# The column sums of WQ behind the first tile's query products, with a new order table

## Chip, cores and metric

The kernel runs on one core of a Trainium2 chip. The metric is the device time of one execution in microseconds (us); several runs are given by their median. The engines are TensorE (PE, with its weight loads PEld), VectorE (DVE), ScalarE (ACT), GpSimd (POOL) and SyncE (SP), which issues most DMAs.

## What is computed

The input x has 2048 rows of 512 columns and is normalised row by row first. Two branches work on the result xn, and the output is x + s * silu(B).

```python
xn = _layernorm(x)                       # no scale, no bias
# A: linear attention, 32 heads of 16
q, k, v = split(xn @ wqkv)               # wqkv: 512 x 1536
pq, pk = phi(q), phi(k)                  # phi(t) = (t + 1 if t > 0 else exp(t)) + 1e-6
s = (pq @ (pk^T v)) / (pq . sum(pk) + 1e-6) @ wo       # per head
# B: shift mixer and MLP
h = gelu(layernorm(xn) @ w1)             # its four column quarters shifted by +1, -1, +2, -2 rows
x1 = xn + shifted(h) @ w2
B = x1 + gelu(layernorm(x1) @ w3) @ w4   # w3: 512 x 1376
out = x + s * silu(B)
```

## The kernel before

**Tiles.** The rows are 16 tiles of 128, in four groups ("quarters") of four tiles; the 512 columns are four chunks of 128. Every fp32 product is made of three products of rounded parts: each operand is split into a rounded high half (`...h`, made on ACT by `rounded`, L522) and a low rest (`...l`, a subtraction on DVE), and `products` (L514) issues high x high, high x low and low x high. Products of one 128 x 128 block by 512 columns go into one PSUM bank. There are eight banks: four of tag `acc`, which the sums `G` (`g`) take, and four of tag `mm`, for everything else.

**Normalisation behind the product.** The first quarter's keys and queries are made from the raw x: `project` (L758) multiplies the transposed x by WK or WQ, 12 products for one tile (four chunks by three). The mean is taken off afterwards: (x - mean) W = xW - mean * (sum of W's rows). `sums` (L766) makes that sum: three additions of the four chunks on DVE (`wqt`), the rounding to `wqmh` on ACT and `wqml` on DVE, two products with a matrix of ones into a PSUM bank (`qsum`), and an ACT copy with sign changed (`qneg`). `query` (L867) then makes `qt` = mean * `qneg` + product on DVE, which is also what frees the tile's PSUM bank, and `feature_q` (L856) goes on with ACT and two DMAs. For the keys it is the same with `ksum`, `wneg` and `kt` (`feature_k`, L828).

**The written order around the change.** At the start come WK's loads, the loads of x, the key products of tiles 0 to 3 (banks k0 to k3), `sums(WK)` and the key features. Then WQ is loaded and split (L1542, L1543) and `sums(WQ, bank("qsum"), qneg)` stands at L1544. Then comes the list `ORD` (L1591): the loads of the second quarter's transposed x (`lu`), the query of tile 0 (`q 0`), `hal`, `x 1`, the query of tile 2 (`q 2`), W1's loads, the sums `g 0`, and so on to the stage `h`, the mixer's first product with W1.

**The emitted order** is made by a planner, `Plan` (L89). Every call of the helpers adds an operation with an estimate of its time; `deadlines` (L259) gives each product of PE a nominal time in written order and each other operation a due time, counted back from the products that need it. `nudged` (L253) then shifts single due times by a table: in `SOONER` (L1745) each pair is an operation's number and a count, and the operation is due by a quarter of a us times the count sooner. `emit` (L296) plays the program through and lets on each engine the operation go that can start first, and among such the one that is due first. PE may take products from up to 12 us ahead. So an operation's place in the queue of its engine follows from the written order, the estimates and the table together, and each engine then works its queue strictly in that order.

Of the kernel before, what the change touches and what calls it, by code (L numbers as in the profile page):

```python
# [430 lines left out]
def linear_attn_gated_by_mixer(  # L431
# [52 lines left out]
    def piece(name, dt=F32):  # L484
        return pl.new("p", name, dt, PIECE)[:, :512]

    def rounds(name):

        return piece(name + "h", F32R), piece(name + "l", F32R)
# [4 lines left out]
    def bank(name):  # L494
        return pl.new("mm", name, F32, 512)[:, :]
# [18 lines left out]
    def products(ps, terms, start=True, stop=True, more=False, behind=None):  # L514

        ms = []
        for sh, sl, mh, ml in terms:
            ms += [(sh, mh), (sh, ml), (sl, mh)]
        for n, (s, m) in enumerate(ms):
            pl.mm(ps, s, m, start and n == 0, stop and n == len(ms) - 1, more=more, behind=None if n else behind)  # L520

    def rounded(hi, lo, full, src=None):  # L522

        pl.act(hi, src or full, AF.Copy)
        split(lo, full, hi)
# [36 lines left out]
    def mean(mv, i):  # L562
        return mv[:, 2 * i:2 * i + 1]
# [191 lines left out]
    def ut(b, c, a, z):  # L755
        return tuple(t[:, a:z] for t in UT[b][c])

    def project(ps, i, ws, cs):  # L758
        b, j = divmod(i, QT)
        a = 2 + j * P  # L760
        products(ps, [ut(b, c, a, a + P) + ws.chunk(c) for c in cs], 0 in cs, NC - 1 in cs)
# [4 lines left out]
    def sums(w, ps, out):  # L766

        t, r = piece(f"{w.name}t"), w.raw
        pl.tt(t, r[0], r[1], ALU.add)
        pl.tt(t, t, r[2], ALU.add)  # L770
        pl.tt(t, t, r[3], ALU.add)
        ts = rounds(w.name + "m")
        rounded(*ts, t)
        for n, v in enumerate(ts):
            pl.mm(ps, onesr.all, v, n == 0, n == 1)
        pl.act(out, ps, AF.Copy, scale=-1.0)
# [79 lines left out]
    def feature_q(i, t):  # L856
        if i >= LATE:
            pl.soon(pl.store(pqd[i].all, t))
            return
        e, r = (piece(f"q{n}{i}") for n in "er")  # L860
        pl.act(by_block(e), by_chunk(t), AF.Relu, scale=col(ns1, i))
        pl.act(by_block(r), by_chunk(t), AF.Relu, scale=col(rs1, i))
        pl.act(e, e, AF.Exp, scale=-1.0)
        pl.soon(pl.store(pqd[i].all, r))
        pl.soon(pl.gather(pqd[i].all, e))

    def query(i):  # L867
        ps = bank(f"q{i}")
        project(ps, i, WQ, range(NC))
        t = piece(f"qt{i}")  # L870
        pl.stt(t, qneg, mean(mv1, i), ps, ALU.mult, ALU.add)
        feature_q(i, t)
# [628 lines left out]
    wneg, qneg = piece("wneg"), piece("qneg")  # L1501
# [39 lines left out]
        feature_k(i, ks[i])  # L1541
    WQ = Weights("wq", wqkv[0])  # L1542
    WQ.split()  # L1543
    sums(WQ, bank("qsum"), qneg)  # L1544
    def scaled(b):
        for j in range(QT):
            if b == 1:
                load_rows(b * QT + j)
            else:
                load_x(b * QT + j)  # L1550
        scale_x(b * QT, QT)
# [54 lines left out]
    def load_w1():  # L1606
        HELD.append(Weights("w1", w1))

    DO = {"wc": lambda: HELD[0].center(by_dma=True), "lu": lambda: load_u(1, 1), "hal": halos, "lw": load_w1, "x": scaled, "kq": keys_queries, "w1": w1_for, "st": stats_of, "g": gram, "mix": mixer, "w2": prepare_w2,
          "a": spread_a, "h": split_halo, "m2": mix2, "u": make_u, "k": key, "q": query, "T": forms_kq}  # L1610
    for what, *args in ORD:
        pl.early = SOON.get(what, 0.0)
# [52 lines left out]
    for b in range(NQ):  # L1665
# [77 lines left out]
                gate(b, QT - 1, r, a, TH, xr=xr[QT - 1], whole=a > 0)  # L1743

    SOONER = (  # L1745
# [18 lines left out]
    )  # L1764
    pl.emit(first=6.0, lead={"p": 14.0, "w": 14.0}, reserve={"p": 20, "w": 1}, window=12.0,
            ahead=6.0, table=SOONER)
# [37 lines left out]
```

## Time and profile before

| what | value |
|---|---|
| median of 3 runs | 503.85 us (503.77 to 504.27) |
| the profiled execution's own time | 503.29 us |
| its span in the profile | 501.5 us |
| granted PE clock, mean | 0.999 |
| PE, PEld busy | 494.1 us, 442.1 us |
| DVE, ACT, POOL busy | 443.4 us, 387.4 us, 82.7 us |
| DMA | 116.69 MB, mean 233 GB/s |

A row of a timeline gives the start in us from the span's start, the duration in us, engine, line, operation, what it writes and reads by the program's names (without buffer numbers), its shape, and in brackets how long the engine stood idle before it and what ended that. In PE's rows the durations overlap, as products are pipelined; the distance from one start to the next tells how fast they go. A row of the view of waits gives who waited for whom, the total in us, how many times, and the longest. Nearly every product is recorded at L151, DVE's additions and subtractions at L198, ACT's work at L173, since helpers issue them; the tile names tell them apart.

### The profile page before, as it was taken

How to read it: one execution, taken by the hardware profiler on the slowest of the kernel's cores; microseconds unless marked ns; L12 is line 12 of the kernel's file. 1: busy time of each engine (PE TensorE's matmuls, PEld its weight loads, DVE VectorE, ACT ScalarE, POOL GpSimd, SP SyncE). 2: the span in 40 equal slices, each digit the busy share in tenths (PEclk: the TensorE clock that was granted, in tenths of full speed). 3: DMA queues.
4: the chain of work that ended last, by engine and by line, in shares of the span. 5: the costliest groups of instructions: out<-in, count | busy, mean ns of one | idle time of the engine just before them, and what ended most of it. 6: DMA issues, size and time to landing. Idle time of an engine off the chain costs nothing.

```text
span 501.5 us, 9471 instructions
## 1 busy us (share of the span) xinstructions
PE 494.1 (99%) x3102; PEld 442.1 (88%) x3102; DVE 443.4 (88%) x944; ACT 387.4 (77%) x859; POOL 82.7 (16%) x97
## 2 busy tenths in 40 slices
PE   8999999999999999999999999999999999999996
PEld 6777887898888888899899999999899998999995
DVE  6899999999699896999999998998899979987364
ACT  6899799766888795977767688957799778977451
POOL 1267123131221022020100011200020200201101
PEclk9999999999999999999999999999999999999999
DMA  7959984479976799989776698988598886896805
GB/s 254 337 138 256 321 256 128 99 157 279 335 219 160 219 307 214 288 232 330 256 250 214 218 326 229 267 255 241 192 275 277 226 207 216 283 329 189 200 1 126
DMA packets 86989, 116.69 MB, mean 233 GB/s; under 512 B 8864, under 2 KB 41148, under 8 KB 86940
## 3 DMA queue, kind: packets, MB, share of 16 engines
q1 hardware_dynamic: 77004, 98.00, 60.2%
q0 software_dynamic: 9936, 18.09, 20.9%
q8 instruction: 24, 0.39, 0.3%
q14 instruction: 25, 0.20, 0.1%
HBM read 73.70 MB, written 32.91 MB: 213 GB/s over the span
## 4 chain that ended last, share of the span: by engine, by line
PE 90%; ACT 4%; DMA 3%; DVE 1%; SPq 0%; issue 0%; ACTq 0%
PE a L151 14%; PE pb L151 10%; PE h L151 9%; PE g L151 9%; PE pbk L151 7%; PE acc L151 6%; PE pe L151 5%; PE pbm L151 5%; PE pbs L151 5%; PE pek L151 3%; PE uc L151 3%; PE pa L151 2%; PE pes L151 2%; PE pem L151 2%; PE pak L151 2%; PE q L151 1%
## 5 line engine op out<-in xcount | busy, mean ns | idle before, releaser
L230 POOL DMA_DIRECT2D th<-in_x x14 | 12.3, 930 | 166.3 <-DMA w_t<-w4t 75.3
L230 POOL DMA_DIRECT2D o<-x x16 | 13.8, 866 | 63.9 <-DVE o L198 42.7
L178 ACT ACT_TABLE_LOAD x18 | 23.1, 1283 | 0.3
L230 POOL DMA_DIRECT2D zacc<-kr x16 | 16.9, 1058 | 35.6 <-DVE kr L208 16.8
L173 ACT ACTIVATE gf<-gf 128x256 f32<-128x256 f32 (+1 forms) x48 | 21.9, 468 | 0.3
L652 POOL TENSOR_TENSOR rs<-w,nhalf 128x4 f32<-128x4 f32 (+2 forms) x10 | 15.8, 1643 | 36.8 <-DVE w L203 36.8
L230 POOL DMA_DIRECT2D e<-x1d x12 | 10.6, 1083 | 63.3 <-DVE e L198 59.7
L173 ACT ACT_TABLE_LOAD x11 | 14.1, 1283 | 2.2 <-issue 1.0
L173 ACT ACTIVATE ht<-ht 128x512 f32<-128x512 f32 x16 | 9.8, 625 | 6.7 <-DVE ht L198 6.2
L208 DVE SCALAR_TENSOR_TENSOR kr<-kt,kr 128x512 f32<-128x512 f32 x16 | 10.9, 684 | 4.3 <-ACT kt L173 4.2
L198 DVE TENSOR_TENSOR th<-th,so 128x512 f32<-128x512 f32 (+1 forms) x17 | 11.0, 655 | 3.6 <-ACT th L173 3.6
L198 DVE TENSOR_TENSOR e<-a,e 128x512 f32<-128x512 f32 (+1 forms) x17 | 9.8, 588 | 4.8 <-PE a L151 4.8
L173 ACT ACTIVATE y<-o,nm,rs 128x512 f32<-128x512 f32 x16 | 11.8, 806 | 2.6 <-DVE nm L208 2.6
L646 DVE BATCH_NORM_STATS2 st<-o 128x6 f32<-128x512 f32 x16 | 10.8, 686 | 3.3 <-DMA o<-x 3.3
L173 ACT ACTIVATE p<-pe 128x256 f32<-128x256 f32 x20 | 7.6, 382 | 7.4 <-PE pe L151 7.4
L198 DVE TENSOR_TENSOR gf<-pa,p 128x256 f32<-128x256 f32 x20 | 8.4, 422 | 5.1 <-PE pa L151 4.5
L173 ACT ACTIVATE x<-x,nm,rs 128x512 f32<-128x512 f32 x16 | 12.9, 804 | 0.0
L173 ACT ACTIVATE th<-e 128x512 f32<-128x512 f32 (+1 forms) x12 | 7.1, 606 | 7.5 <-DVE e L198 7.4
L198 DVE TENSOR_TENSOR ht<-h,abc 128x512 f32<-128x512 f32 x16 | 10.9, 686 | 1.2 <-PE h L151 1.0
L173 ACT ACTIVATE p<-pb 128x256 f32<-128x256 f32 x20 | 7.5, 377 | 5.4 <-PE pb L151 5.3
L208 DVE SCALAR_TENSOR_TENSOR pq<-pq,rd 128x512 f32<-128x512 f32 x16 | 10.9, 678 | 0.1
L1413 DVE TENSOR_REDUCE den<-qz 128x32 f32<-128x512 f32 x16 | 10.8, 681 | 0.1
(1868 smaller groups left out, 2288.5 us busy)
## 6 DMA issues: line engine op xcount, KB each, us to landing
w_s<-in_w SPq DMA_DIRECT2D x34, 256.0 KB, 5.1
w_t<-w4t SPq DMA_DIRECT2D x26, 256.0 KB, 6.2
w_b<-w4d SPq DMA_DIRECT2D x24, 256.0 KB, 4.7
x<-in_x SPq DMA_DIRECT2D x16, 256.0 KB, 6.2
zacc<-kr POOLq DMA_DIRECT2D x16, 256.0 KB, 4.9
o<-x POOLq DMA_DIRECT2D x16, 256.0 KB, 4.7
x1d<-o SPq DMA_DIRECT2D x16, 256.0 KB, 3.2
xt<-in_xt SPq DMA_DIRECT2D x15, 256.0 KB, 6.3
```

The source lines that it names most:

```text
L151: lambda: nc.tensor.matmul(out.get(), lhs.get(), rhs.get(), start=start, stop=stop, skip_group_check=more))
L173: nc.scalar.activation(out.get(), src.get(), func, scale=get(scale), **kw)
L178: op.warm = lambda: nc.scalar.activation(self.scr[1].get(), self.scr[0].get(), func)
L198: self.vec(eng, out, [a, b], lambda: self.e(eng).tensor_tensor(out.get(), a.get(), b.get(), op=op), True)
L208: lambda: self.nc.vector.scalar_tensor_tensor(out.get(), a.get(), get(s), b.get(), op0=op0, op1=op1),
L230: lambda: self.nc.gpsimd.dma_start(out.get(), get(src), accum_op=ALU.add))
L646: pl.add("DVE", .62, .69, [xv], [st], lambda: nc.vector.bn_stats(st.get(), xv.get()))
L652: lambda: g.tensor_tensor(out.get(), src.get(), nh.get(), op=ALU.pow))
L1413: pl.add("DVE", .6, .68, [t], [den], lambda: nc.vector.tensor_reduce(den.get(), t.get().rearrange("p (h d) -> p h d", d=DH), axis=AX.X, op ...
```

## The change

The call of `sums` for WQ is taken out of the main line and put into `query`, for tile 0, between the tile's 12 products and the DVE operation that uses `qneg`. The operations of the loads `lu` and of the 12 products so get numbers lower by 8, those of the sum higher by 16; all others keep theirs. The table `SOONER` is replaced: 163 pairs for 181. 35 pairs are the same in both, 68 operations have another count, 78 are nudged only before and 60 only after. The first lines of both tables are shown.

```diff
     def query(i):
         ps = bank(f"q{i}")
         project(ps, i, WQ, range(NC))
+        if i == 0:
+            sums(WQ, bank("qsum"), qneg)
         t = piece(f"qt{i}")
         pl.stt(t, qneg, mean(mv1, i), ps, ALU.mult, ALU.add)
         feature_q(i, t)
...
     WQ = Weights("wq", wqkv[0])
     WQ.split()
-    sums(WQ, bank("qsum"), qneg)
     def scaled(b):
...
     SOONER = (
-        0, 16, 2, 377, 19, 8894, 26, 3270, 31, 261, 34, 64, 36, 38809, 42, 3243, 43, 155, 55, 33, 62, 32, 72, 16,
-        83, 16, 86, 58, 87, 64, 94, 64, 97, 64, 117, -64, 121, 9, 134, 13, 152, 16, 165, 8, 168, 35, 170, 568,
-        171, 512, 174, 31, 176, 16, 178, 32, 199, 32, 203, -32, 213, 31, 253, -16, 266, 70, 277, 3, 278, 57,
...
+        2, 309, 19, 38290, 23, 20, 24, 16, 26, 2469, 31, 130, 36, 38310, 42, 1201, 43, 154, 54, 5, 55, 36, 62, 32,
+        70, 16, 83, 15, 86, 58, 89, 8, 97, 130, 121, 18, 127, 114, 170, 248, 171, 515, 174, 62, 176, 19, 177, 64,
+        191, 32, 203, -71, 213, 10, 253, -83, 273, 61, 278, 28, 280, 33, 297, 16, 305, -32, 316, 457, 320, 83,
...
     )
```

28 rows, old and new, of the table SOONER are left out of this document.

## The prediction

> **What bounds the kernel now.** I read the page first, then the view of TensorE's waits, then the engines' timelines from 17 to 37 us, and last the busy time by stretches.
>
> ```profile
> span 501.5 us, 9471 instructions
> PE 494.1 (99%) x3102; PEld 442.1 (88%) x3102; DVE 443.4 (88%) x944; ACT 387.4 (77%) x859; POOL 82.7 (16%) x97
> PE 90%; ACT 4%; DMA 3%; DVE 1%; SPq 0%; issue 0%; ACTq 0%
> ```
> TensorE (PE) is busy for 99% of the span and makes 90% of the chain that ended last. Time can come only from places where PE stands still. The view of PE's waits has two rows:
>
> ```profile
> PE warm L151 <- POOL ones L548: 1.7, 1, 1.7
> PE qsum L151 <- ACT wqmh L173: 0.8, 1, 0.8
> ```
> The first is the start. The second is the sum that the change moves: the first `qsum` product waits for `wqmh`, the rounded sum of WQ's rows. PE's timeline there:
>
> ```profile
> 20.64 0.39 PE L151 MATMUL q<-wq_3h,u_3l 128*128 128x512 f32 x1
> 20.87 0.40 PE L151 MATMUL q<-wq_0h,u_0h 128*128 128x512 f32 x1
> ...
> 21.58 0.39 PE L151 MATMUL q<-wq_1h,u_1h 128*128 128x512 f32 x1
> 22.79 0.50 PE L151 MATMUL qsum<-wqmh,onesr 128*128 128x512 f32 x1 [0.82 <-ACT wqmh L173]
> 23.13 0.40 PE L151 MATMUL q<-wq_1l,u_1h 128*128 128x512 f32 x1
> 23.36 0.40 PE L151 MATMUL q<-wq_1h,u_1l 128*128 128x512 f32 x1
> ...
> 24.75 0.40 PE L151 MATMUL q<-wq_3h,u_3l 128*128 128x512 f32 x1
> 24.98 0.39 PE L151 MATMUL qsum<-wqml,onesr 128*128 128x512 f32 x1
> ```
> Products of 512 columns start 0.23 us apart (20.64, 20.87). After 21.58 the next would start at 21.81; it starts at 22.79, **0.98 us late**, and the one behind it follows after 0.34 instead of 0.23, 0.11 more. So the stall costs 0.98 + 0.11 = 1.09 us. Two things in these rows matter for the change. The `qsum` product already stands behind all twelve products of the first query tile (the last of them at 20.64) and four of the next: the emitting order is not the written one. And eight products that had long been ready stood behind it (23.13 to 24.75). What made it late:
>
> ```profile
> 19.05 0.74 DVE L208 SCALAR_TENSOR_TENSOR kt<-wneg,mv,k 128x512 f32<-128x512 f32 x1
> ...
> 20.59 0.69 DVE L198 TENSOR_TENSOR wqt<-wqt,wq_s 128x512 f32<-128x512 f32 x1
> 21.19 0.15 DVE L203 TENSOR_SCALAR mv<-sx 128x1 f32<-128x1 f32 x1
> 21.25 0.68 DVE L198 TENSOR_TENSOR x0l<-x,x0h 128x512 fp32r<-128x512 f32 x1
> 21.85 0.74 DVE L208 SCALAR_TENSOR_TENSOR kt<-wneg,mv,k 128x512 f32<-128x512 f32 x1
> ...
> 23.83 0.69 DVE L198 TENSOR_TENSOR wqml<-wqt,wqmh 128x512 fp32r<-128x512 f32 x1
> ```
>
> ```profile
> 21.50 0.62 ACT L173 ACTIVATE sq<-x 128x512 f32<-128x512 f32 x1
> ...
> 22.12 0.62 ACT L173 ACTIVATE wqmh<-wqt 128x512 fp32r<-128x512 f32 x1
> ...
> 25.42 0.60 ACT L173 ACTIVATE qneg<-qsum 128x512 f32<-128x512 f32 x1 [0.56 <-PE qsum L151]
> ```
> `wqmh` ends at 22.12 + 0.62 = 22.74. There is a second condition that the waits view does not name. PSUM has four `mm` banks; k0 to k3 hold them all, q0 and q2 take the first two that VectorE (DVE) frees with a `kt` (q2, at 20.87, behind the `kt` of 19.05), and the sum takes the next: the `kt` at 21.85 ends at 22.59. An earlier `wqmh` alone would have won 22.74 - 22.59 = 0.15 us.
>
> **The change part by part.**
>
> The eight operations of the sum stay: three additions and `wqml` on DVE (0.69 us each), `wqmh` and `qneg` on ScalarE (ACT, 0.62 and 0.60), two products (0.23). No DMA, table load or tile is added. Busy time: 0.
>
> The move itself. In the written order the sum goes behind 12 products, so its due times fall by 12 x 0.23 = 2.8 us, as do those of the additions that feed it. PE's emission already had it later than that, so the move says only that the additions may go later. Best case: both `qsum` products come behind the eight ready products of the second tile, which without the stall end their starts at 24.75 - 1.09 = 23.66. Then `wqmh` (22.74) and the bank (22.59) are long there: gain 1.09 us. Worst case: the product is again emitted the moment the planner thinks it ready, and the stall stays: 0. These are the two ends for this edit.
>
> What is late next. A PE that is 1.09 us earlier at 25 us runs into operands that do not come earlier with it, since they come from ACT and DVE:
>
> ```profile
> 24.00:34.00 10.00, 10.00 (x45) 7.92 (x45) 9.47 (x26) 9.25 (x21) 6.11 (x6) 1.00 0.67 163
> 34.00:44.00 10.00, 10.00 (x45) 7.81 (x43) 9.78 (x21) 9.55 (x27) 8.64 (x7) 1.00 0.84 175
> 44.00:54.00 10.00, 10.00 (x45) 8.12 (x45) 9.96 (x19) 10.00 (x26) 3.47 (x4) 1.00 1.09 287
> ```
> The columns behind the stretch are its sum, PE, PEld, DVE, ACT and POOL. DVE is busy 9.47, 9.78 and 9.96 of 10 us and ACT 9.25, 9.55 and 10.00: no room to be earlier, only to be ordered otherwise. The next operands that are just in time:
>
> ```profile
> 29.25 0.61 ACT L173 ACTIVATE k2h<-kr 128x512 fp32r<-128x512 f32 x1
> ...
> 32.08 0.61 ACT L173 ACTIVATE w1mh<-w1t 128x512 fp32r<-128x512 f32 x1
> ...
> 34.97 0.61 ACT L173 ACTIVATE k1h<-kr 128x512 fp32r<-128x512 f32 x1
> ```
>
> ```profile
> 30.44 0.85 PE L151 MATMUL g<-k2h,x2h 128*128 128x512 f32 x3
> 31.12 0.40 PE L151 MATMUL g<-k2l,x2h 128*128 128x512 f32 x1
> ...
> 33.10 0.40 PE L151 MATMUL w1m<-w1mh,onesr 128*128 128x512 f32 x1
> ...
> 35.99 0.87 PE L151 MATMUL g<-k1h,x1h 128*128 128x512 f32 x3
> ```
> `k2h` ends at 29.86 and its first product starts at 30.44, 0.58 later; `w1mh` 32.69 and 33.10: 0.41; `k1h` 35.58 and 35.99: 0.41. From `wqmh`'s end to its product passed 22.79 - 22.74 = 0.05, so a product can follow its operand by that. The lead that survives all three is 0.41 - 0.05 = 0.36 us. Of 1.09 us won at 22 us, 0.73 would be lost again by 36 us.
>
> One place of the Trainium skill speaks on whether a stall of PE lasts at all: "TensorE: Matmul & The Clock Gate", section "Back-to-back issue gap", gives a sustained 131 ns per 512-column product in a real kernel against about 216 for a single one. By that PE would make up 1.09 us in about 11 products, and removing the stall would bring nothing: 503.85. The rows above disagree: behind the stall the products start 0.23 us apart as before it (23.13, 23.36), so nothing is made up.
>
> The new table. It has 163 pairs in place of 181; 35 are as before, the others nudge due times by new amounts, all over the program. It issues nothing new, but it may exchange neighbours on every queue, SP's first loads included (entries 19 to 43), and it was drawn up for another order. The trace of before cannot show what it does. Bounds from the nearest rows: a gain is limited by PE's other halts, of which these are the largest:
>
> ```profile
> 242.27 0.40 PE L151 MATMUL acc<-w_0h,f_0l 128*128 128x512 f32 x1
> 242.66 0.39 PE L151 MATMUL pb<-yt40h,w_b 128*128 128x256 f32 x1
> 242.88 0.28 PE L151 MATMUL pb<-yt40l,w_b 128*128 128x256 f32 x1
> ```
>
> ```profile
> 379.57 0.28 PE L151 MATMUL a<-w_t,f_1a 128*128 128x256 f32 x1
> 379.95 0.39 PE L151 MATMUL pe<-yb222h,w_s1h 128*128 128x256 f32 x1
> 380.17 0.28 PE L151 MATMUL pe<-yb222l,w_s1h 128*128 128x256 f32 x1
> ```
> At 242.27 a 512-column product is followed after 0.39 and the next 256-column one after 0.22 instead of 0.23 and 0.12: 0.26 us. At 379.57 it is 0.38 and 0.22 instead of 0.12 twice: 0.36 us. Together 0.62. A loss is bounded by the price of one misplaced product, the 1.09 us of `qsum`; two new ones of its kind make 2.2. I take 0, the middle of -0.6 and +2.2 being no better founded: before shows one such wait in 500 us, so the nearest row for a finished order is few waits.
>
> Sum: 503.85 - 0.36 + 0 = **503.5 us**. The profiled execution took 503.29 us, 501.5 of it span; by the same sum it would take 502.9. The median of the three runs, 503.85, stands 0.56 above it, and the forecast is set against the median.
>
> **The rivals.**
>
> *Little is won (forecast).* The stall goes or shrinks, the lead is lost at the next just-in-time operands, 503.5. Or the change does not do what it says: as PE's queue had the sum behind the first tile already, the stall stays, 503.85. Both are within 0.2% (1.0 us), which is about what a measurement of this kernel can tell from no change. For it: the surviving 0.36 and the full DVE and ACT. Against: a new order can break up exactly those three places. Chance 0.40, of which 0.02 for PE making up a stall (503.85).
>
> *The lead is kept: faster.* The table puts `k2h`, `w1mh` and `k1h` early enough by letting DVE's additions of `wqt` go later, and the halts at 242 and 380 go too: 503.85 - 1.09 - 0.62 = 502.1; the lead alone is 502.8. For it: the additions are what stood ahead of the others on DVE at 20.59. Against: 1.0 us needs nearly all of the 1.09, through a stretch where DVE and ACT are full for 30 us. Chance 0.28.
>
> *The moved additions make key products late: slower.* Place: DVE's queue from 23.8 to 31 us. There stand `wqml` and what `k2l` needs, and PE's product on `k2l` follows at 31.12. Its row:
>
> ```profile
> 29.90 0.69 DVE L208 SCALAR_TENSOR_TENSOR k2l<-kr,k2h 128x512 fp32r<-128x512 f32 x1 [0.39 <-ACT k2h L173]
> ```
> `k2l` ends at 30.59, 0.53 ahead of its product. Starts of DVE instructions of this kind are 0.60 apart (20.59 to 21.19). If all of the three additions and `wqml` slide by their 2.8 us into this stretch, `k2l` comes 4 x 0.60 = 2.4 us later, less the slack of 0.53 - 0.05: +1.9, 505.8; with three of them +1.3, 505.2. It decides from two additions on (1.2 us against a slack of 0.48). Against it: what leaves DVE's queue at 18 to 21 us makes room there for others, so the total does not grow. With a like misplacement elsewhere in the run, by the price of two waits, 506.0. Chance 0.32.
>
> **How the numbers follow.** Within 0.2%: 0.40; faster: 0.28; slower: 0.32. Signs both ways hold most of the chance; the forecast's own range is 502.9 to 504.3 (its two ends with 0.5 of spread between runs: 503.77 to 504.27). The whole range leaves out a tenth on each side: from 502.1, the fast rival's price, to 506.0, the slow one's.
>
> **What would show it.**
>
> ```profile
> 42.74 0.40 PE L151 MATMUL h<-u_0h,w_0h 128*128 128x512 f32 x1
> ```
> This is the first product of `h`, the next stage. The move right: no wait of PE on `wqmh`, and eight products of the second query tile without a hole. The term 0.36 right: new short waits of PE at `k2h`, `k2l`, `w1mh` or `k1h` between 28 and 37 us, and the first product of `h` earlier than 42.74 by 0.2 to 0.5 us. Wrong to the fast side: that product earlier by 0.9 or more and no later wait. Wrong to the slow side: rows of PE waiting of 0.5 us and more on DVE or a DMA, anywhere. The table's 0 is wrong if the time from the first `h` product to the end differs from now by more than 0.6.

## Result and profile after

In six runs of each kernel, the changed kernel took **502.07 us** (501.63 to 502.89), the one before 504.06 (503.77 to 504.44). The ratio is **0.9963, 95% interval 0.9953 to 0.9973**: faster by 0.37%, 1.9 us. That is not the forecast case (within 0.2%); it is the size of the fast rival (502.1). The experiments show that its mechanism was another. Three of all executions below took 812 to 984 us, whatever the kernel, and stand in no ratio.

The device time is longer than the span of the instructions in the profile, and no view shows what lies between the two. In before this part is 1.96 to 1.98 us (medians of its executions beside three groups of runs), in after 1.72 and 1.71. So some 0.25 of the 1.9 us lies where no row below can show it.

The page of the changed kernel follows; its profiled execution took 502.89 us, the slowest of the six.

```profile
span 501.2 us, 9464 instructions
PE 494.3 (99%) x3102; PEld 442.2 (88%) x3102; DVE 440.9 (88%) x944; ACT 388.9 (78%) x859; POOL 84.9 (17%) x97
PE 88%; DMA 8%; SPq 1%; ACT 1%; issue 0%; DVE 0%; POOL 0%; DVEq 0%
PE a L151 15%; PE pb L151 11%; PE h L151 9%; PE pbk L151 7%; PE g L151 7%; PE acc L151 6%; PE pe L151 6%; DMA w1t<-in_w 5%; PE pbm L151 5%; PE pbs L151 4%; PE uc L151 3%; PE pek L151 3%; PE pa L151 3%; PE pem L151 2%; PE pes L151 2%; PE pak L151 2%
```

Busy times are as before. New is the chain that ended last: DMA has 8% of it instead of 3%, and 5% are the gathers of W1 (`w1t<-in_w`). The view of PE's waits (total, times, longest in us) says the same:

```profile
PE w1m L151 <- ACT w1mh L173: 0.6, 1, 0.6
PE h L151 <- ACT w_1h L173: 0.2, 1, 0.2
```

The wait of `qsum` on `wqmh` is gone, and two new ones stand at W1. PE's timeline at the sum (start, duration):

```profile
23.56 0.40 PE L151 MATMUL q<-wq_3l,u_3h 128*128 128x512 f32 x1
23.81 0.51 PE L151 MATMUL qsum<-wqmh,onesr 128*128 128x512 f32 x1
24.15 0.40 PE L151 MATMUL q<-wq_3h,u_3l 128*128 128x512 f32 x1
```

```profile
23.14 0.62 ACT L173 ACTIVATE wqmh<-wqt 128x512 fp32r<-128x512 f32 x1
```

Seven of the eight ready products now stand ahead of the sum. `wqmh` has slid too, from 22.74 to 23.76 at its end, so the product still only just finds it: 23.81 is 0.02 behind the usual distance and the next 0.11 more. In this execution the stall of 1.09 us shrank to 0.13. But the stall differs from execution to execution with the same queues, counted as the prediction did (hole and 0.11 behind it): in the seven executions that have before's queues up to 60 us (before, before_again, before_tail, before_to60, before_60_349, before_mid, before_late) it was 1.09, 0.45, 0.69, 1.16, 1.10, 0.35 and 0 us (median 0.69), in the four with after's (after, after_again, after_to60, after_tail) 0.13, 0.44, 0.38 and 0. It depends on when PE comes to the product, and so on its earlier halts: in before PE is ready for the product at 21.81 and waits until 22.79, in before_late it comes to it only at 24.17, when `wqmh` has been ready since 23.90, and doesn't wait. The 1.09 us of the prediction stand near the top of this range.

Then the stage `h`:

```profile
43.02 0.40 PE L151 MATMUL h<-u_0h,w_0h 128*128 128x512 f32 x1
...
43.95 0.63 PE L151 MATMUL h<-u_0h,w_0l 128*128 128x512 f32 x2
44.80 0.49 PE L151 MATMUL h<-u_1h,w_1h 128*128 128x512 f32 x1 [0.22 <-ACT w_1h L173]
```

Here the first `h` product is not earlier than 42.74 but 0.28 later, and the one on `w_1h` stands 0.38 late behind two products (0.85 instead of 0.47). Yet the kernel is faster.

**One measure for all runs.** For every execution the table gives PE's *standing time*: the start of a product less the usual distances of all products ahead of it (0.232 us for 512 columns, 0.118 for 256, 0.112 and 0.027 for the two small kinds). Two places are met with the same work done in all kernels: the first `h` product (167 products, 36.25 us of work) and the 271st product (60.18). The third place is at 481 us of work. "End" is from PE's last product's end to DVE's last. The letters tell whose queues (before's, after's) run up to 60 us, up to 490 us, and to the end.

| run | queues | at first `h` | at 60 of work | 60 to 481 | end |
|---|---|---|---|---|---|
| before | b b b | 6.48 | 6.56 | 2.50 | 1.87 |
| before_again | b b b | 6.66 | 6.73 | 3.54 | 1.87 |
| before_tail | b b a | 6.67 | 6.62 | 2.42 | 1.33 |
| before_to60 | b a a | 6.95 | 6.98 | 1.95 | 1.33 |
| after_to60 | a b b | 5.61 | 6.32 | 2.53 | 1.85 |
| after_tail | a a b | 5.95 | 6.48 | 1.65 | 1.84 |
| after | a a a | 6.77 | 7.27 | 1.98 | 1.33 |
| after_again | a a a | 6.02 | 6.70 | 1.94 | 1.34 |

Up to 60 us of work, the new queues end level with the old ones, within the spread of single executions. The middle is 0.4 to 0.9 us shorter and the end 0.54, wherever after's queues run there. (3.54 holds a single wait of 0.95 us at 312 us that no other execution has.)

### The profile page after: what moved, and what is told of

The parts are those of the page before. It is cut to its first block, busy times and chain, and to the rows that moved or that the text cites. A ratio compares the mean times of both kernels' runs of the same rounds, so it can differ in the third digit from the quotient of the medians.

```text
span 501.2 us, 9464 instructions
## 1 busy us (share of the span) xinstructions
PE 494.3 (99%) x3102; PEld 442.2 (88%) x3102; DVE 440.9 (88%) x944; ACT 388.9 (78%) x859; POOL 84.9 (17%) x97
## 4 chain that ended last, share of the span: by engine, by line
PE 88%; DMA 8%; SPq 1%; ACT 1%; issue 0%; DVE 0%; POOL 0%; DVEq 0%
PE a L151 15%; PE pb L151 11%; PE h L151 9%; PE pbk L151 7%; PE g L151 7%; PE acc L151 6%; PE pe L151 6%; DMA w1t<-in_w 5%; PE pbm L151 5%; PE pbs L151 4%; PE uc L151 3%; PE pek L151 3%; PE pa L151 3%; PE pem L151 2%; PE pes L151 2%; PE pak L151 2%
## 5 line engine op out<-in xcount | busy, mean ns | idle before, releaser
L208 DVE SCALAR_TENSOR_TENSOR pq<-pq,qr 128x512 f32<-128x512 f32 x12 | 8.2, 686 | 3.9 <-ACT pq L173 3.8
L198 DVE TENSOR_TENSOR gf<-pb,p 128x256 f32<-128x256 f32 x20 | 8.4, 418 | 3.1 <-PE pb L151 3.0
L208 DVE SCALAR_TENSOR_TENSOR qz<-pq,zb 128x512 f32<-128x512 f32 x16 | 10.7, 684 | 0.2
```

What stands on the lines that cost most here:

```text
L198: self.vec(eng, out, [a, b], lambda: self.e(eng).tensor_tensor(out.get(), a.get(), b.get(), op=op), True)
L208: lambda: self.nc.vector.scalar_tensor_tensor(out.get(), a.get(), get(s), b.get(), op0=op0, op1=op1),
```

## Experiments

**Both kernels again**, without an edit.

> The kernel before, unchanged, for a second profile. Its profiled execution took 503.29 us, 0.77 below the median of its six timed runs (504.06), so the one profile may miss a hole that most executions have. Theory A (the whole difference is the wait on the sum): the same picture, one wait of PE of 0.8 us on wqmh and no other of 0.3 us or more, time 503.8 to 504.4. Theory B (executions differ in how late the chain of loads behind w1m lands): a further wait near w1m (33 us) or the first h products (43 us) of 0.3 to 1 us.

> The changed kernel, unchanged, for a second profile: the first was its slowest execution (502.89 against a median of 502.07). Theory A (the wait on the sum is gone and its 1.09 us is kept): no wait on w1mh or w_1h in this execution, the first h product at 41.8 to 42.2, time near 502.0, ratio 0.996. Theory B (the lead is used up by operands that do not come sooner, and the gain lies later in the run): first h product again at 42.7 to 43.0, ratio 0.996 all the same, and fewer holes after 50 us than before. In both the start is about 0.4 us slower than before, as in the first profile.

before: 504.65 in one run, beside a median of 503.80 in 21. after: 501.81 (501.55 to 502.90), ratio 0.9968 (0.9955 to 0.9980). The gain repeats. In this execution of before the view of waits has 0.2 us of `qsum` on `wqmh` in place of 0.8. In this execution of after the wait on `w1mh` is absent and the first `h` product starts at 42.28; the loss at `w_1h` is there again, and a wait of 0.2 us of `qsum` on `wqmh`.

**The product's move alone, in before's queues.** A line in the planner holds an operation back until another one is emitted. The first `qsum` product (184) goes right in front of the second (185), behind the eight ready products; all else is before's, the sum's additions and `wqmh` too.

```diff
+HELD, BEHIND = (184,), (185,)
...
+    def go(self, op, held=[]):
+        held.append(op) if op.order in HELD else [o.emit() for o in (held if op.order in BEHIND else []) + [op]]
+        held[:] = [] if op.order in BEHIND else held
...
-            op.emit()
+            self.go(op)
```

> The kernel before with one instruction moved: the first qsum product is queued right in front of the second, behind the eight products of the second query tile; table and all else as before. My forecast's reasoning: the wait on wqmh goes (1.09 us), 0.73 of it is lost again at k2h, w1mh and k1h, 0.36 stays: ratio 0.9993, first h product at 42.4. Theory A (lead kept): 1.0 to 1.1 us, ratio 0.998. Theory B (gain lies later in the run, in the table): ratio 0.999 to 1.000.

503.62 us, ratio 0.9996 (0.9986 to 1.0006): nothing that can be measured. PE's timeline shows why:

```profile
23.96 0.39 PE L151 MATMUL q<-wq_3h,u_3l 128*128 128x512 f32 x1
24.19 0.39 PE L151 MATMUL qsum<-wqmh,onesr 128*128 128x512 f32 x1
24.95 0.51 PE L151 MATMUL qsum<-wqml,onesr 128*128 128x512 f32 x1 [0.37 <-DVE wqml L198]
25.29 0.63 PE L151 MATMUL g<-k0h,x0h 128*128 128x512 f32 x2
```

The first product has no hole; the second waits for `wqml`: 0.76 and 0.34 instead of 0.23 twice, so 0.64 us of standing are back in the next row. Whether anything is left can't be told from this one execution: its standing time at the first `h` product is 6.55, within the 6.48 to 8.29 (median 6.81) of the seven executions with before's own start.

**The move undone, in after's queues.** The sum's first product stands five products sooner; the same edit, with

```diff
+HELD, BEHIND = (247, 248, 249, 250, 251), (252,)
```

> The changed kernel with the first qsum product queued five products sooner, so that PE waits for wqmh for about 1.1 us again; all else as changed. Theory A (the gain is this wait): half of the gain goes, 1.1 us more than the changed kernel, ratio to before 0.998. My forecast's reasoning (0.36 of it survives): 0.4 us more than the changed kernel, ratio 0.997. Theory B (gain lies later): ratio 0.996, as the changed kernel.

503.10 us, ratio to before 0.9984 (0.9975 to 0.9993), so 0.8 us above after_again's ratio:

```profile
22.69 0.39 PE L151 MATMUL q<-wq_1h,u_1l 128*128 128x512 f32 x1
23.83 0.50 PE L151 MATMUL qsum<-wqmh,onesr 128*128 128x512 f32 x1 [0.75 <-ACT wqmh L173]
24.17 0.39 PE L151 MATMUL q<-wq_2h,u_2h 128*128 128x512 f32 x1
```

The stall is back at 0.91 + 0.11 = 1.02 us, and the standing time at 60 us of work is 7.71, against 6.70 in after_again. So in the new queues the sum's place is worth about what its stall costs. Since these queues end the first 60 us level with before's, they must lose elsewhere in them what they win at the sum.

**Where along the run the gain lies.** For the next kernels the planner takes its operations from a list: the order of one kernel up to a given PE product, then that of the other. In the traces the order of PE, ACT, DVE and POOL is that of the one kernel up to the change, and that of the other from there.

```diff
+QUEUE = ...   # numbers of all operations, in the order to emit
-                for op in cands:
+                for op in (o for o in cands if o.order == QUEUE[len(done)]):
```

after_to60 changes from after's order to before's at the 233rd operation of PE (60 us in the planner's time), before_to60 the other way; before_tail and after_tail change at the 3037th (490.8 us).

> The queues of the changed kernel up to its 233rd PE operation (about 60 us, behind the stage h and the first products of the next), from there those of the kernel before. Theory A (the gain is made at the moved sum and in the first 60 us): ratio 0.996 to 0.997. Theory B (the gain is made later, by the table): PE's idle time at that point is 6.70 and 7.27 us in the two profiles of the changed kernel against 6.56 and 6.73 before, so ratio 1.000 to 1.001.

> The other half: the queues of the kernel before, with the sum in its old place, up to the 233rd PE operation, from there those of the changed kernel. Theory A: ratio 0.999 to 1.000. Theory B: the whole gain or a little more, ratio 0.995 to 0.9965, with the wait of 0.8 us on wqmh still in the profile.

> The kernel before up to its 3037th PE operation (490.8 us), from there the queues of the changed kernel, in which the left half of the last tile's product ends ahead of the right half. The end of the last DVE operation lies 1.87 us behind PE's last product before and 1.33 behind it in the changed kernel. Theory B with the end as a part of it: 0.5 us less, ratio 0.999. Theory A: 1.000.

> The changed kernel up to its 3037th PE operation, from there the queues of the kernel before, whose last steps are one longer. Theory B with the end as a part of it: 0.5 us of the gain gone, ratio 0.997. Theory A: the whole gain, 0.996.

| kernel | median, us | ratio to before, 95% |
|---|---|---|
| after_to60: only the first 60 us new | 503.56 | 0.9996 (0.9986 to 1.0006) |
| before_to60: all but the first 60 us new | 502.06 | 0.9969 (0.9956 to 0.9981) |
| before_tail: only the last 10 us new | 502.81 | 0.9985 (0.9975 to 0.9996) |
| after_tail: all but the last 10 us new | 502.38 | 0.9977 (0.9969 to 0.9986) |

This settles the main question. The first 60 us, which hold the moved sum, bring 0.2 us (-0.3 to 0.7); the rest, to which the change gives only another order, brings 1.6 (1.0 to 2.2), the last 10 us alone 0.8 (0.2 to 1.3). after_tail agrees: without the new end, 0.5 us less is won than in after_again (0.9977 against 0.9968).

The spans alone (medians) are 501.7 us for before beside these runs, and 501.8, 500.4, 501.0 and 500.7 for the four kernels in the order of the table. Within its span the kernel with only the first 60 us new is thus not shorter than before, and the rest brings 1.3 us. Outside the span after_to60 and before_to60 both have about 1.7 us and before_tail 1.8, against 1.97 in before; why, no run shows.

The timeline of before's end, and then of after's and before_tail's:

```profile
496.46 0.28 PE L151 MATMUL a<-w_9h,f_9l 128*128 128x256 f32 x1
...
496.83 0.42 DVE L198 TENSOR_TENSOR e<-a,e 128x256 f32<-128x256 f32 x1
497.28 0.42 ACT L173 ACTIVATE th<-e 128x256 f32<-128x256 f32 x1 [1.28 <-DVE e L198]
497.73 0.42 DVE L198 TENSOR_TENSOR th<-th,so 128x256 f32<-128x256 f32 x1 [0.48 <-ACT th L173]
498.19 0.42 DVE L198 TENSOR_TENSOR th<-th,xr 128x256 f32<-128x256 f32 x1
```

```profile
496.67 0.28 PE L151 MATMUL a4x<-w_9h,f_9l 128*128 128x256 f32 x1
496.98 0.38 ACT L173 ACTIVATE th<-a4x 128x256 f32<-128x256 f32 x1 [0.92 <-PE a4x L151]
497.40 0.42 DVE L198 TENSOR_TENSOR th<-th,so 128x256 f32<-128x256 f32 x1 [0.40 <-ACT th L173]
497.86 0.42 DVE L198 TENSOR_TENSOR th<-th,xr 128x256 f32<-128x256 f32 x1
```

```profile
496.47 0.28 PE L151 MATMUL a4x<-w_9h,f_9l 128*128 128x256 f32 x1
...
497.66 0.42 DVE L198 TENSOR_TENSOR th<-th,xr 128x256 f32<-128x256 f32 x1
```

The last tile's two column halves have different work behind PE. The half `a` needs an addition on DVE (`e`) ahead of ACT's `th`; the half `a4x` goes to ACT at once. Before ends with `a`: 498.61 - 496.74 = 1.87 us. After ends with `a4x`: 498.28 - 496.95 = 1.33. Nothing runs beside this, so the 0.54 us are time, and before_tail has them.

**Where in the middle.** The list changes at PE's 1985th (349 us) and 2309th operation (393 us).

> The queues of before with only the stretch from TensorE's 233rd to its 1985th operation (60 to 349 us) in the order of after. Theory: nothing, ratio 1.000 (after has a hole of 0.35 us at 341 us that before has not, before one of 0.26 at 242 that after has not). Rival (the gain in the middle is spread): 0.45 us below before, ratio 0.9991.

> The queues of before with only the stretch from TensorE's 1985th to its 2309th operation (349 to 393 us) in the order of after. Theory (what the new order wins in the middle is mainly the holes between 377.7 and 380 us): 0.6 to 0.7 us below before, ratio 0.9987, and TensorE without a hole of 0.2 us or more between 360 and 393 us. Rival (the gain in the middle is spread over many small exchanges): 0.1 to 0.2 us below before, ratio 0.9997.

> The queues of before up to TensorE's 1985th operation (349 us), then those of after to the end. Theory (the holes at 378 to 380 us and the last operations carry the gain): 0.65 + 0.54 = 1.2 us below before, ratio 0.9976. Rival (the gain in the middle is spread evenly from 60 to 490 us): 0.54 and a third of 0.7, so 0.75 us below before, ratio 0.9985.

before_60_349: 503.55, 0.9994 (0.9981 to 1.0008). before_mid (349 to 393 us new): 503.36, 0.9992 (0.9981 to 1.0003). before_late (all from 349 us new): 503.02, 0.9981 (0.9971 to 0.9992). None parts its theory from its rival, and before_60_349 lies nearer its rival (0.9991). The profile is sharper than these times. In before, the halt at 379.57 that the prediction quoted belongs to a group:

```profile
377.74 0.28 PE L151 MATMUL pa<-yb212h,w_al 128*128 128x256 f32 x1
377.96 0.39 PE L151 MATMUL pe<-yt12h,w_s0h 128*128 128x256 f32 x1
378.19 0.28 PE L151 MATMUL pe<-yt12l,w_s0h 128*128 128x256 f32 x1
...
378.78 0.36 PE L151 MATMUL pb<-yt22h,w_s0h 128*128 128x256 f32 x1
378.98 0.28 PE L151 MATMUL pb<-yt22l,w_s0h 128*128 128x256 f32 x1
```

```profile
378.59 0.73 ACT L173 ACTIVATE qr<-qv,rs 128x512 f32<-128x512 f32 x1
379.20 0.42 ACT L173 ACTIVATE f_2a<-gf 128x256 fp32r<-128x256 f32 x1
379.52 0.38 ACT L173 ACTIVATE p<-pe 128x256 f32<-128x256 f32 x1
```

With the 0.12 us of a 256-column product as measure, the holes are 0.10, 0.11, 0.08, 0.26 and 0.10 us: 0.65 together. All six executions with before's queues in this stretch have them (0.65 to 0.70), none of the eight with after's has one over 0.04 between them. The largest, 0.26, is in front of the product on `yb222h` at 379.95. The view of that tile names ACT's `p` as what ended 0.3 us of waiting; `p<-pe` stands behind `qr` and `f_2a`. In after:

```profile
379.80 0.39 ACT L173 ACTIVATE p<-pe 128x256 f32<-128x256 f32 x1
...
380.79 0.41 ACT L173 ACTIVATE f_2a<-gf 128x256 fp32r<-128x256 f32 x1
```

```profile
380.31 0.28 PE L151 MATMUL a<-w_t,f_1a 128*128 128x256 f32 x1
380.43 0.28 PE L151 MATMUL pe<-yb222h,w_s1h 128*128 128x256 f32 x1
```

`f_2a` has gone behind `p<-pe`, and PE goes on after 0.12. That fits the last two holes, 0.36 together; what made the first three is not shown, as other neighbours have changed places there too. In before_mid the group is gone as well, but its joint at 349 us makes new holes:

```profile
352.07 0.39 PE L151 MATMUL a<-w_3h,f_3h 128*128 128x512 f32 x1
352.56 0.39 PE L151 MATMUL pbs<-m_t4h,q 128*128 128x256 f32 x1
```

Here a 512-column product is followed after 0.49 instead of 0.23. With what follows this halt and a smaller one at 349.25, the standing time grows by 0.6 us across the joint, nearly what was won. before_late has the same joint. So the two cut out the group, but their times do not price it.

**What the new order loses at W1.** In after the second `w1m` product starts 1.38 us behind the first (1.27 in after_again), in before 0.93 (34.03 - 33.10). From it hangs a chain: ACT copies `w1t`, four DMAs bring it into `w_s`, ACT rounds `w_1h`, PE multiplies. The last kernel puts three PE products behind the second `w1m` product, and one ACT operation (`kr` of the fourth tile) behind the copy `w1t`; all else is after's.

```diff
+def behind(o, x):
+    QUEUE.remove(o); QUEUE.insert(QUEUE.index(x) + 1, o)
+for o in (399, 307, 306): behind(o, 315)
+behind(161, 316)
```

> After with three products of TensorE put behind the second w1m product, and one ScalarE operation (kr of the fourth tile) behind the copy w1t that this product feeds. Theory (what after is ahead at the first h product is lost at the third one, because w_1h comes through a chain of fixed length that starts at the second w1m product): w_1h 0.5 to 0.6 us sooner against the first w1m product, no hole of over 0.2 us in front of the h product on w_1h, 0.4 to 0.6 us below after: about 501.3, ratio to before 0.9957. Rival (something else sets w_1h, such as the transfers that carry the chain): w_1h and the time as in after, 501.8, ratio 0.9968.

501.75 us (501.42 to 502.54), ratio to before 0.9959 (0.9943 to 0.9974). The rows of after_again, and then of this kernel, for PE:

```profile
32.52 0.39 PE L151 MATMUL w1m<-w1mh,onesr 128*128 128x512 f32 x1
...
33.79 0.39 PE L151 MATMUL w1m<-w1ml,onesr 128*128 128x512 f32 x1
...
42.28 0.40 PE L151 MATMUL h<-u_0h,w_0h 128*128 128x512 f32 x1
...
43.21 0.64 PE L151 MATMUL h<-u_0h,w_0l 128*128 128x512 f32 x2
44.25 0.50 PE L151 MATMUL h<-u_1h,w_1h 128*128 128x512 f32 x1 [0.40 <-ACT w_1h L173]
```

```profile
32.28 0.39 PE L151 MATMUL w1m<-w1mh,onesr 128*128 128x512 f32 x1
...
33.02 0.50 PE L151 MATMUL w1m<-w1ml,onesr 128*128 128x512 f32 x1
...
42.31 0.40 PE L151 MATMUL h<-u_0h,w_0h 128*128 128x512 f32 x1
...
43.24 0.64 PE L151 MATMUL h<-u_0h,w_0l 128*128 128x512 f32 x2
43.71 0.40 PE L151 MATMUL h<-u_1h,w_1h 128*128 128x512 f32 x1
```

and for ACT's `w_1h` and the four transfers into `w_s` (shortest, median and longest), in the same order:

```profile
43.57 0.63 ACT L173 ACTIVATE w_1h<-w_s 128x512 fp32r<-128x512 f32 x1 [0.81 <-DMA w_s<-w1t]
DMA to landing us min/median/max: 3.5/6.5/8.9
```

```profile
42.56 0.61 ACT L173 ACTIVATE w_1h<-w_s 128x512 fp32r<-128x512 f32 x1
DMA to landing us min/median/max: 3.6/5.5/7.7
```

The first `h` product starts at the same time in both, and `w_1h` 1.0 us sooner. The hole of 0.57 us in front of its product is gone, and the standing time at 60 us of work is 6.06, against 6.70. That PE stands there for `w_1h`, and that the order at `w1m` moves it, is shown.

That the chain has a fixed length, as the theory said, is not so. `w_1h` needs the third of the four transfers. In this kernel it is issued 0.66 us sooner than in after_again (35.59 against 36.25) but lands 1.97 sooner (41.57 against 43.54): from issue to landing it takes 5.98 us in place of 7.29. In the four executions of after's queues it takes 7.03 to 7.31 us, in the seven of before's 6.61 to 6.77. So after loses at `w_1h` by the later product and by 0.3 to 0.7 us of slower transfers; why they are slower stays open. Of the 1.97 us, 1.31 are the rival's, the transfer itself. An estimate from these rows says that the 0.66 would have been enough: a landing at 42.88 and ACT's 0.63 make 43.51, ahead of the product at 43.71.

That the kernel is faster than after is likely: the ratios to before are 0.9959 and 0.9968, some 0.5 us, and the spans 499.8 against 500.1 and 500.35 (medians), but the intervals overlap.

## Where the prediction was right and where it was wrong

The time, 502.07 us, came out at the low edge of the whole range (502.1) and outside the forecast's own range (502.9 to 504.3). That the edge held is luck: it was the price of the rival "the lead is kept", whose mechanism did not come.

**The stall of 1.09 us.** It was read rightly from its rows, but from one execution: with the same queues it is 0 to 1.16 us, 0.69 in the middle, and the forecast was set against the median of the runs. That it would go was right, though by seven products instead of eight, with `wqmh` 1.02 us later. after_sum_sooner shows what a stall of 1.02 us costs there, some 0.8. That the move alone is worth between 0 and 1.09 held in before_hold, near 0.

**"What is late next".** The mechanism was right, the places mostly not. The prediction looked at `k2h`, `w1mh` and `k1h`, operands that come just in time by their own row. Of these only `w1mh` held PE up, in two of after's four executions, for 0.6 and 0.2 us. In before_hold 0.64 us were lost at once, on `wqml`, the operand of the sum's own second product. In after the lead went at `w_1h`, three steps behind `w1m`. The four executions with after's unaltered first 60 us stand at 5.61 to 6.77 us at the first `h` product (median 5.99), the seven with before's at 6.48 to 8.29 (median 6.81): a lead of some 0.8. By 60 us of work after's have lost 0.50, 0.68, 0.71 and 0.53 of it; six of the seven others lost 0.09 or less. The 0.36 for the surviving part is neither confirmed nor refuted: after_to60 measured 0.2 (-0.3 to 0.7), and within the span nothing (501.8 against 501.7).

**"The new table ... I take 0".** This is the step that failed. So everything behind 60 us was given 0, with -0.6 as the best; before_to60 measured -1.6 (-2.2 to -1.0), 1.3 of it within the span. Two things were missing. The bound counted PE's largest halts singly, 0.26 and 0.36; the second was part of a group of 0.65. And it counted PE's halts only ("Time can come only from places where PE stands still"): the 1.87 us from PE's last product to DVE's last are no halt of PE, and the prediction read no row for them. A different order of the last two halves takes 0.54 from them. "1.09 for a misplaced product" as the bound of a loss was right in kind, as `w_1h` shows, but the new order does not place worse on the whole.

**The rivals.** "The lead is kept" gave 502.1 as 1.09 + 0.62. The number came true and the mechanism didn't: the first 60 us bring 0.2 us or nothing, and the gain lies behind them, at the halt at 380 that was a part of the 0.62, at the end, and outside the span. "Moved additions make `k2l` late" did not happen: no execution of after waits there. Nor did PE make up anything: behind the sum's stall in after_sum_sooner it keeps the distance of 0.23 us, and the loss is there at 60 us of work.

**What would show it.** The test for the table was the time from the first `h` product to the end, with 0.6 as limit. By the device times it is 503.29 - 42.74 = 460.55 before and 502.89 - 43.02 = 459.87 after, a difference of 0.68; by the spans it is 501.5 - 42.74 = 458.76 and 501.2 - 43.02 = 458.18, a difference of 0.58. The test thus stood at its limit, as the 0.5 lost at `w_1h` behind that product hid as much of the gain. It took before_to60 to show that the 0 was wrong.

**What stays open.** Of the 1.6 us behind 60 us, the end carries 0.54 by the rows, and the group at 378 us 0.65 by the rows without a time of its own. Some 0.26 lies outside the span (1.97 us in before, 1.71 in before_to60, medians); after_to60 has as much of it (1.70), so it belongs to no stretch of the order, and its cause is open. The rest is within the interval; before's hole at 242 us, which the prediction counted, is no fixed part of its queues, as before_tail, with the same queues there, has none.

## What to carry to other kernels

Where PE is full, price each removed wait by the next operand of the same chain that is just in time, and follow it through its DMAs: behind a `w1m` product placed 0.34 to 0.45 us later, and transfers 0.3 to 0.7 us slower, PE lost 0.5 to 0.7 us at `w_1h`, ten microseconds on. Take the size of a wait from several executions: this one was 0 to 1.16 us with the same queues. When a change comes with a new order for the whole program, don't set the order to zero: add up the holes of PE over whole stretches, and read what runs from PE's last product to the end, since here each step of it was time. Then cut the run in two and let each half have one of the two orders; that separated the parts here when the profiles of single executions could not.

## Not expected of the hardware

The landing of chained transfers differs from execution to execution, and where they land late the start of the kernel follows them. ACT's `w1mh` needs the last of the chained gathers of W1. In before that lands at 30.83, and `w1mh` starts at 32.08 without waiting for it; in one execution of before_60_349 (the same queues up to there) it lands at 34.07:

```profile
34.09 0.63 ACT L173 ACTIVATE w1mh<-w1t 128x512 fp32r<-128x512 f32 x1 [0.78 <-DMA w1t<-in_w]
```

That execution took 505.84 us, the slowest of its twelve, whose median is 503.55. One profile therefore can't price a term of half a us in the first 60 us: after's own profile shows a later `h` than before's, and three other executions of its first queues an earlier one.
